# FNet mixing with a squared-ReLU feed-forward: E's coefficients by way of DRAM, weights rounded in two operations

## The chip, the cores and the metric

One Trainium2 chip, one of its cores. The metric is the device time of one execution in microseconds (us); the profile adds one execution taken by the hardware profiler, whose times are those of the tables below. The engines are TensorE (PE for its products, PEld for its weight loads), VectorE (DVE), ScalarE (ACT), GpSimd (POOL) and SyncE (SP), which here only issues transfers.

## The reference

x has 8 sequences of 3008 rows and 256 columns, in float32; w_in is 256 x 2048 and w_out 2048 x 256. Both weights come as float64 arrays, since a float32 array is multiplied by a float64 scalar.

```python
X = np.fft.fft(x, axis=1)
X = np.fft.fft(X, axis=2)
h = X.real.reshape(8 * 3008, 256) @ w_in
g = np.maximum(h, 0.0) ** 2
out = g @ w_out
```

## The kernel before

**The transform.** The real part of the two-dimensional transform is written with symmetries. For each sequence the rows of x are folded and multiplied by cosine and sine tables along the sequence; the results are P (tile Pt) and Q (tile Qt), 128 partitions by 1505 frequencies, where the partitions are half of the 256 columns. The transform along the columns is not carried out on them: it is folded into the weights instead. w_in is multiplied once by the column tables cosd and sind, which gives G1 and G2, 128 x 2048 each, and the first product of the feed-forward is then G1 with P plus or minus G2 with Q: the sum serves a frequency k, the difference its mirror.

**E.** One column of x, the middle one (number 128), does not fit into the 128 partitions. Its transform along the sequence is a single row of 1505 numbers for each sequence, called E (in DRAM as e_dram, spread over all partitions in the tile ew). For each of the 2048 hidden units it needs one coefficient, which is the last partition (127) of G2: row 127 there is w_in summed with alternating signs. The tile gE, 128 x 16, holds these coefficients with the hidden unit on the partition, so that DVE can add E times its coefficient to hP (`front`, L1019, and `front_half`/`split_half`, L1001). To bring row 127 of G2 onto the partitions, `ends_of` (L352) multiplies 128 x 128 pieces of G2 with the last column of the identity, and `keep_ends` (L359) halves the result on DVE into gE (L360). A product in float32 is two instructions for each of two halves of the hidden units: 4 for each of 8 weight groups j, 32 in all.

**Halving and doubling.** gE holds half of each coefficient, and E twice its value. For the first sequence `f_e` (L562) copies the column with a sign of 1 or -1 into `lone`; for the other seven, whose columns are loaded element by element into the tile xe (`load_columns`, L456), POOL doubles xe (L475).

**Rounding the weights.** The weights arrive as float64, as pairs of 32-bit words, and are turned into float32 by `convert` (L289): DVE takes the sign (`begin`, L299), ACT scales the high word (L306) and rounds the low word in two steps (L307 adds 2^23 so that the fraction is rounded away, L308 takes 2^23 off again), DVE shifts the high word (`halves`, L314), and POOL adds the two (`product`, L323). It runs 8 times for w_in, 8 times for w_out and twice more at the end, when two groups of w_out are read anew. The tokens TS, PW, H and PR in the order below are these four parts.

**Steps.** A step is one block of 252 (or 246) frequencies with one group j of 256 hidden units; there are 8 sequences x 6 blocks x 8 groups = 384 steps. A step takes 8 instructions for hP and hQ (L1015), DVE's sum with E and the sum and difference with hQ into g (L1019, L1023, L1024; for the first steps L1001 to L1004), ACT's relu and square (L1028, L1031) and POOL's sums for a fast product with w_out (L1043 to L1060). Two steps later PE multiplies with w_out and with sums of its parts, wsum (`run`, L1080), into six banks F0 to F2 and S0 to S2. After the 8 groups of a block `gather` (L1122) forms the block's output c from the banks: `early` copies a part of F to SBUF on ACT; `upper`, `lower`, `joins` and `last_joins` are sums on DVE, placed between the steps; `back` is a copy on ACT. In the last block (`final`) one sum is formed on POOL instead, and the last two groups are multiplied plainly in `finish` (L1181), which adds them to c (L1191).

**Order.** No scheduler moves anything: each engine runs its instructions in the order in which the program writes them. The first 10 steps, the building of G1, G2 and gE, the rounding of the weights and the sums of w_out are interleaved by a list of tokens written by hand, ORDER (L1423). In it pgC3 and pgD3 are the products for group 3 of G1 and G2, GC3 and GD3 ACT's copies (`keep_win`, L348), fe3 and gE3 the two parts of the coefficients, f3a and f3b the two halves of step 3's first product, d3a and d3b what DVE does with them (L1001, L1003, L1004), rl and sq relu and square, bk the plain product with w_out of the first 8 steps, lc four loads of xe, sc and su the sums of w_out, restP and restQ the rest of P and Q. SP issues its transfers in the same order, among them the raw weights: when the rounding of one (H) has freed its buffer, `load_more` issues the next. A wait on SP holds all that stands behind it. hP and hQ share two banks of PSUM, so that a step's products wait for DVE to have read an earlier one.

A stretch of ORDER that matters for the steps 1, 2 and 6:

```python
'... pgC2 GD1 TSw0 rl0 fe1 f1b H3 PWw0 f1a gE1 PR3 '
'd1b pgD2 GC2 d1a GD2 keep f2b TS4 rl1 pgD3 Hw0 fe2 GD3 pgC3 sq0 gE2 PRw0 d2b ...'
'gE5 PRw3 pgD6 d5b sq3 f5a GC6 H7 lc bk3 GD6 rl4 TSw4 PR7 PWw4 d5a pgD7 restP rl5 fe6 Hw4 f6b GD7 sq4 f6a '
'gE6 PRw4 d6b sq5 sc0a fe7 pgC7 gE7 TSw5 bk4 TSw6 PWw5 restQ GC7 d6a spl lc ...'
```

Of the kernel before, what the change touches and what calls it, by code (L numbers as in the profile page):

```python
# [15 lines left out]
P = 128  # L16
# [68 lines left out]
def kernel(  # L85
# [119 lines left out]
    gE = const.tile([P, NFC], F32, name="gE")  # L205

# [39 lines left out]
    ramp = const.tile([P, 2], F32, name="ramp")  # L246
    nc.vector.memset(ramp[:, 0:1], 2.0 ** 23)
    nc.vector.memset(ramp[:, 1:2], -2.0 ** 23)
# [40 lines left out]
    def convert(raw, dst, k):  # L289
# [12 lines left out]
        def powers():  # L302
            if high is None:
                return
            m = st["m"] = scratch()
            act(high.bitcast(F32), high.bitcast(F32), AF.Copy, scale=2.0 ** -112)  # L306
            act(m, low, AF.Relu, bias=ramp[:, 0:1], scale=2.0 ** -29)  # L307
            act(m.bitcast(U32), m, AF.Relu, bias=ramp[:, 1:2], scale=1.0)  # L308
# [39 lines left out]
    def keep_win(j, side, pg):  # L348
        to, v = (G1, G2)[side].rearrange("p (h j f) -> j p h f", h=2, j=NJ)[j], pg.rearrange("p (h f) -> p h f", h=2)
        nc.scalar.copy(to, v)  # L350

    def ends_of(j):  # L352
        ps = psd.tile([P, CH], F32, name="pe", tag="d")
        for h in range(2):
            fc = j + NJ * h
            nc.tensor.matmul(ps[:, h:h + 1], G2[:, fc * P:(fc + 1) * P], last, start=True, stop=True)
        return ps

    def keep_ends(j, ps):  # L359
        nc.vector.tensor_scalar_mul(gE[:, j::NJ], ps[:, 0:2], 0.5)  # L360
# [99 lines left out]
    def fold_columns():  # L460
# [12 lines left out]
        def begin():  # L473
            assert not COLUMNS
            gt(out=xe, in0=xe, in1=xe, op=ADD)  # L475
# [56 lines left out]
    def fold(t):  # L532
# [28 lines left out]
        def f_e():  # L561
            nc.scalar.mul(lone[r, 2 * t:2 * t + 2, P - 1:], w[r, :, H:H + 1], -1.0 if TILES[t][0] else 1.0)  # L562
# [552 lines left out]
    def gather_plain(n):  # L1115

        c = new_c(n)
        for h, nm in enumerate(("mA", "mB")):
            nc.scalar.copy(c[:, 2 * n * h:2 * n * (h + 1)], acc[nm][:, 0:2 * n])
        return c  # L1120

    def gather(n, final):  # L1122
# [10 lines left out]
        def early():  # L1133
            nc.scalar.copy(cf[:, 1:3], F1[:, 0:2])
            nc.scalar.copy(cf[:, 0], F2[:, 0])

        def upper():
            tt(out=o[:, 3], in0=F0[:, 0], in1=cf[:, 2], op=SUB)
            tt(out=o[:, 4:6], in0=F0[:, 1:3], in1=wide(cf[:, 2:3]), op=ADD)
            tt(out=o[:, 1], in0=F1[:, 2], in1=cf[:, 1], op=ADD)  # L1140
            tt(out=o[:, 2], in0=F1[:, 0], in1=cf[:, 0], op=SUB)
            tt(out=o[:, 0], in0=F2[:, 1], in1=cf[:, 0], op=ADD)

        def lower():
# [5 lines left out]
            if final:  # L1150
                gt(out=cs[:, 0], in0=vt[:, 0], in1=vt[:, 1], op=SUB)
                gt(out=o[:, 4], in0=o[:, 4], in1=cs[:, 0], op=ADD)
# [526 lines left out]
```

## Time and profile before

| | |
|---|---|
| median of 3 runs | 1870.71 us (1870.31 to 1871.78) |
| the profiled execution | 1872.4 us |
| its span, first to last instruction | 1870.6 us |
| granted TensorE clock | 0.998 |
| PE busy | 1856.8 us, 99% |
| DVE busy | 1472.0 us, 79% |
| POOL busy | 1463.9 us, 78% |
| ACT busy | 1086.8 us, 58% |
| products of `ends_of` (L356) | 32, from 33.6 to 78.0 us |
| DVE's copies of gE (L360) | 8, 161 ns (median) |
| ACT's second rounding step (L308) | 18, 722 ns each |
| transfers on SP's queue | 151166 packets, 66.79 MB |

A row of a timeline or a group names engine, line of the program, operation, and the tiles written and read; in square brackets stands the idle time of the engine just before and what ended it. The rows of busy time by stretch name the stretch in us from the start of the span, its length, the busy time and number of instructions of PE, PEld, DVE, ACT and POOL, the granted clock, the mean busy share of the DMA engines and the GB/s that they moved. An engine's busy time counts overlapping instructions once. A transfer's line on SP is its issue; the transfer itself goes on after it.

### The profile page before, as it was taken

To read this page: it belongs to the slowest core of one execution; us is meant where nothing else is said; L and a number is where in the kernel's file an instruction comes from. 1 tells how busy PE (TensorE), PEld (TensorE's weight loads), DVE (VectorE), ACT (ScalarE), POOL (GpSimd) and SP (SyncE) were. 2 spreads that over 40 slices of the span, in tenths; PEclk is the share of its full clock that TensorE was granted. 3 is DMA by queue.
4 is the path that set the end of the run, shared out by engine and by line. 5 is a ranking of instruction groups with operands and counts; after the bars stand their busy time and mean duration, and the time that the engine had idled before them with its cause. 6 is when DMAs were issued, how large, how long until landed. Compare 5 with 4: busy or idle time off the path is not lost.

```text
span 1870.6 us, 34033 instructions
## 1 busy us (share of the span) xinstructions
PE 1856.8 (99%) x11384; PEld 1752.6 (94%) x11384; DVE 1472.0 (79%) x3488; ACT 1086.8 (58%) x1609; POOL 1463.9 (78%) x2140
## 2 busy tenths in 40 slices
PE   9999999999999999999999999999999999999998
PEld 7689999999999999999999999999999999999997
DVE  7788877887788877878787787788877887767666
ACT  5876645666465655566556564566645666444454
POOL 3479878878787887888878887788877878788885
PEclk9999999999999999999999999999999999999999
DMA  7432001100011111111011110111001100000010
GB/s 198 119 55 46 15 21 46 51 23 21 21 51 40 29 23 32 32 46 31 16 32 46 37 26 15 43 48 34 15 20 43 37 15 20 18 20 15 20 43 23
DMA packets 151886, 69.51 MB, mean 37 GB/s; under 512 B 131207, under 2 KB 142945, under 8 KB 151712
## 3 DMA queue, kind: packets, MB, share of 16 engines
q1 hardware_dynamic: 151166, 66.79, 14.4%
q8 instruction: 91, 1.49, 0.3%
q14 instruction: 83, 0.68, 0.1%
q0 software_dynamic: 416, 0.43, 0.1%
q10 hardware_dynamic: 130, 0.12, 0.0%
HBM read 42.59 MB, written 24.69 MB: 36 GB/s over the span
## 4 chain that ended last, share of the span: by engine, by line
PE 95%; DVE 3%; DMA 1%; ACT 1%; issue 0%; POOL 0%; DVEq 0%; POOLq 0%; ACTq 0%
PE F L1080 33%; PE S L1080 23%; PE hP L1015 17%; PE hQ L1015 17%; PE pd L745 2%; PE pd L868 1%; PE pd L842 1%; PE pg L345 1%; DVE wsum L390 0%; DMA cosT<-in_cos_s_dram 0%; PE fin L1188 0%; DVE he L1019 0%; PE mA L1109 0%; PE mB L1109 0%; DVE he L1001 0%
## 5 line engine op out<-in xcount | busy, mean ns | idle before, releaser
L1028 ACT ACTIVATE g<-g 128x1008 f32<-128x1008 f32 (+1 forms) x384 | 399.4, 1040 | 301.7 <-DVE g L1024 280.2
L1019 DVE SCALAR_TENSOR_TENSOR he<-ew,gE,hP 128x252 f32<-128x252 f32 (+1 forms) x748 | 321.4, 471 | 286.5 <-PE hP L1015 286.5
L1031 ACT ACTIVATE g<-g 128x1008 f32<-128x1008 f32 (+1 forms) x384 | 399.4, 1040 | 12.0
L1015 PE MATMUL hP<-Pt,G 128*128 128x252 f32 (+1 forms) x1496 | 379.0, 376 | 3.4 <-DVE w L670 1.4
L1015 PE MATMUL hQ<-Qt,G 128*128 128x252 f32 (+3 forms) x1496 | 379.1, 376 | 0.3 <-DVE g L1024 0.3
L1080 PE MATMUL F<-s,wsum 128*128 128x168 f32 (+1 forms) x1496 | 335.3, 306 | 0.0
L1015 PEld LDWEIGHTS hQ<-Qt,G 128*128 128x128 f32 (+1 forms) x1496 | 281.8, 190 | 37.7 <-issue 2.6
L1080 PE MATMUL F<-g,wout 128*128 128x168 f32 (+1 forms) x1496 | 304.0, 305 | 0.0
L1053 POOL TENSOR_TENSOR s<-g 128x168 f32<-128x168 f32 (+1 forms) x187 | 101.2, 541 | 256.2 <-ACT g L1031 122.4
L1015 PEld LDWEIGHTS hP<-Pt,G 128*128 128x128 f32 x1496 | 265.9, 190 | 22.6 <-DVE fs L606 1.6
L1023 DVE TENSOR_TENSOR g<-he,hQ 128x504 f32<-128x504 f32 (+1 forms) x374 | 253.0, 676 | 41.2 <-DVE he L1019 2.9
L1080 PE MATMUL S<-s,wout 128*128 128x168 f32 (+1 forms) x1496 | 280.6, 306 | 0.1
L1080 PE MATMUL S<-s,wsum 128*128 128x168 f32 (+1 forms) x1496 | 273.7, 306 | 0.4 <-DVE c L1165 0.4
L1080 PE MATMUL F<-g,wsum 128*128 128x168 f32 (+1 forms) x1496 | 273.5, 305 | 0.0
L1024 DVE TENSOR_TENSOR g<-he,hQ 128x504 f32<-128x504 f32 (+1 forms) x374 | 250.7, 670 | 0.0
L1080 PEld LDWEIGHTS S<-s,wsum 128*128 128x128 f32 x1496 | 239.1, 190 | 9.0 <-issue 0.9
L1080 PEld LDWEIGHTS F<-s,wsum 128*128 128x128 f32 x1496 | 247.5, 190 | 0.0
L1080 PEld LDWEIGHTS F<-g,wsum 128*128 128x128 f32 x1496 | 239.3, 190 | 8.1
L1080 PEld LDWEIGHTS F<-g,wout 128*128 128x128 f32 x1496 | 239.3, 190 | 0.0
L1080 PEld LDWEIGHTS S<-s,wout 128*128 128x128 f32 x1496 | 231.0, 190 | 1.0 <-POOL s L1060 0.6
L1059 POOL TENSOR_TENSOR s<-s 128x336 f32<-128x336 f32 (+1 forms) x187 | 168.0, 898 | 14.7
L1056 POOL TENSOR_TENSOR s<-s 128x336 f32<-128x336 f32 (+1 forms) x187 | 168.0, 898 | 14.7
(232 smaller groups left out, 2520.2 us busy)
## 6 DMA issues: line engine op xcount, KB each, us to landing
out_dram<-os SPq DMA_DIRECT2D x376, 56.0 KB
xt<-in_x_dram SPq DMA_DIRECT2D x39, 384.0 KB
xt<-in_x_dram SPq DMA_DIRECT2D x63, 128.0 KB
raw<-in_moe_w_out_dram SPq DMA_DIRECT2D x20, 256.0 KB
ew<-e_dram SPq DMA_DIRECT2D x39, 126.0 KB
out_dram<-os SPq DMA_DIRECT2D x288, 7.0 KB
raw<-in_moe_w_in_dram SPq DMA_DIRECT2D x16, 256.0 KB
xt<-in_x_dram SPq DMA_DIRECT2D x2, 512.0 KB
```

Of the source, the lines that this page charges most:

```text
L345: nc.tensor.matmul(pg, tab[:, i], win[j][:, i], start=i == 0, stop=i == 1)
L745: nc.tensor.matmul(ps[0:w.shape[-1]], w, part_of(cosT if lone_e else tab, t)[0:rows, kp, PLACE[t]:PLACE[t] + NC[kp][c]], start=t == ts[0] ...
L1015: nc.tensor.matmul(to[:, h, 0:n], w[:, fs], v[:, ks], start=h == 0, stop=True, skip_group_check=True)
L1019: nc.vector.scalar_tensor_tensor(out=t[:, h, 0:n], in0=window[b, k0][:, 0:n], scalar=gE[:, fc:fc + 1], in1=hP[:, h, 0:n], op0=ALU.mult, op ...
L1023: tt(out=g[:, :, 0:n], in0=t[:, :, 0:n], in1=hQ[:, :, 0:n], op=ALU.add)
L1024: tt(out=g[:, :, n:2 * n][:, :, ::-1], in0=t[:, :, 0:n], in1=hQ[:, :, 0:n], op=ALU.subtract)
L1028: act(g[:, :, 0:2 * n], g[:, :, 0:2 * n], AF.Relu)
L1031: act(g[:, :, 0:2 * n], g[:, :, 0:2 * n], AF.Square)
L1053: gt(out=s[:, 11], in0=b2[:, 0], in1=b1[:, 0], op=SUB)
L1056: gt(out=s[:, 4:6], in0=s[:, 4:6], in1=s[:, 10:11].to_broadcast([P, 2, tb]), op=SUB)
L1059: gt(out=s[:, 6:9:2], in0=s[:, 2:4], in1=s[:, 6:8], op=ADD)
L1080: nc.tensor.matmul(acc[nm][:, slot, 0:tb], w, v, start=q == 0 and nm not in begun, stop=q == end - 1, skip_group_check=True)
```

## The change

Row 127 of G2 no longer goes through TensorE. After ACT's copy of a group of G2, SP writes the group's 256 coefficients from that partition to a small array in DRAM, g_dram, and then reads them back with the hidden unit on the partition, straight into gE (`take_ends`). `ends_of` and `keep_ends` go. In ORDER the read stands right behind the copy: "GD1 gE1".

gE is no longer halved, so E is: `f_e` copies with 0.5 or -0.5, and POOL's doubling of xe goes.

The rounding takes two operations of ACT: L307 writes the rounded low word as an integer at once, without taking 2^23 off. The sum with the high word is then one binary exponent too high, so the weights are twice as large. w_in's factor of two is taken out in the copies of G1 and G2, w_out's where the block's output is gathered: ACT's copies there are scaled by 0.5, and DVE's sums with a bank of PSUM become SCALAR_TENSOR_TENSOR, which halves one operand and adds. The last block takes the same way through `gather` as the others.

```diff
@@ -203,6 +203,7 @@
     G1 = const.tile([P, F], F32, name="G1")
     G2 = const.tile([P, F], F32, name="G2")
     gE = const.tile([P, NFC], F32, name="gE")
+    g_dram = dp.tile([NJ, 2 * P], F32, name="g_dram")
 
     def load_table(tab, src, tiles, queue=nc.sync):
@@ -243,9 +244,9 @@
     for c in range(2):
         nc.vector.tensor_scalar(out=sind[:, c, P - 1:], in0=evens, scalar1=2.0, scalar2=-1.0,
                                 op0=ALU.mult, op1=ALU.add)
-    ramp = const.tile([P, 2], F32, name="ramp")
-    nc.vector.memset(ramp[:, 0:1], 2.0 ** 23)
-    nc.vector.memset(ramp[:, 1:2], -2.0 ** 23)
+    ramp = const.tile([P, 1], F32, name="ramp")
+    nc.vector.memset(ramp, 2.0 ** 23)
+    FACTOR = 2.0 if moe_w_in.dtype != F32 else 1.0
 
 
     def awake(n):
@@ -304,8 +305,7 @@
                 return
             m = st["m"] = scratch()
             act(high.bitcast(F32), high.bitcast(F32), AF.Copy, scale=2.0 ** -112)
-            act(m, low, AF.Relu, bias=ramp[:, 0:1], scale=2.0 ** -29)
-            act(m.bitcast(U32), m, AF.Relu, bias=ramp[:, 1:2], scale=1.0)
+            act(m.bitcast(U32), low, AF.Relu, bias=ramp, scale=2.0 ** -29)
 
         def halves():
             if high is None:
@@ -347,17 +347,13 @@
 
     def keep_win(j, side, pg):
         to, v = (G1, G2)[side].rearrange("p (h j f) -> j p h f", h=2, j=NJ)[j], pg.rearrange("p (h f) -> p h f", h=2)
-        nc.scalar.copy(to, v)
-
-    def ends_of(j):
-        ps = psd.tile([P, CH], F32, name="pe", tag="d")
-        for h in range(2):
-            fc = j + NJ * h
-            nc.tensor.matmul(ps[:, h:h + 1], G2[:, fc * P:(fc + 1) * P], last, start=True, stop=True)
-        return ps
-
-    def keep_ends(j, ps):
-        nc.vector.tensor_scalar_mul(gE[:, j::NJ], ps[:, 0:2], 0.5)
+        nc.scalar.mul(to, v, 1.0 / FACTOR)
+        if side:
+            nc.sync.dma_start(out=g_dram[j:j + 1].rearrange("o (h f) -> o h f", h=2),
+                              in_=G2[P - 1:P].rearrange("o (h j f) -> j o h f", h=2, j=NJ)[j])
+
+    def take_ends(j):
+        nc.sync.dma_start(out=gE[:, j::NJ], in_=g_dram[j].rearrange("(h f) -> f h", h=2))
 
     def weights(D, row):
 
@@ -472,7 +468,6 @@
 
         def begin():
             assert not COLUMNS
-            gt(out=xe, in0=xe, in1=xe, op=ADD)
             s = hp.tile([P, 2, NL, NE], F32, name="es", tag="es", bufs=1)
             gt(out=s, in0=xe[:, 0::2], in1=xe[:, 1::2], op=ADD)
             for kp in range(2):
@@ -559,7 +554,7 @@
                 tt(out=w[r, kp, part], in0=v[r, 0, part], in1=v[r, 1, part], op=SUB if kp else ADD)
 
         def f_e():
-            nc.scalar.mul(lone[r, 2 * t:2 * t + 2, P - 1:], w[r, :, H:H + 1], -1.0 if TILES[t][0] else 1.0)
+            nc.scalar.mul(lone[r, 2 * t:2 * t + 2, P - 1:], w[r, :, H:H + 1], -0.5 if TILES[t][0] else 0.5)
 
         return [f_s, f_d, f_sc, f_dc, lambda: (f_w(PART[0]), f_e()), lambda: f_w(PART[1])]
 
@@ -1116,10 +1111,13 @@
 
         c = new_c(n)
         for h, nm in enumerate(("mA", "mB")):
-            nc.scalar.copy(c[:, 2 * n * h:2 * n * (h + 1)], acc[nm][:, 0:2 * n])
+            nc.scalar.mul(c[:, 2 * n * h:2 * n * (h + 1)], acc[nm][:, 0:2 * n], 1.0 / FACTOR)
         return c
 
-    def gather(n, final):
+    def scaled(out, in0, in1, op=ADD):
+        mix(out=out, in0=in0, scalar=1.0 / FACTOR, in1=in1, op0=ALU.mult, op1=op)
+
+    def gather(n):
 
         tb = 2 * n // 3
         c = new_c(n)
@@ -1131,15 +1129,15 @@
         wide = lambda v: v.to_broadcast([P, 2, tb])
 
         def early():
-            nc.scalar.copy(cf[:, 1:3], F1[:, 0:2])
-            nc.scalar.copy(cf[:, 0], F2[:, 0])
+            nc.scalar.mul(cf[:, 1:3], F1[:, 0:2], 1.0 / FACTOR)
+            nc.scalar.mul(cf[:, 0], F2[:, 0], 1.0 / FACTOR)
 
         def upper():
-            tt(out=o[:, 3], in0=F0[:, 0], in1=cf[:, 2], op=SUB)
-            tt(out=o[:, 4:6], in0=F0[:, 1:3], in1=wide(cf[:, 2:3]), op=ADD)
-            tt(out=o[:, 1], in0=F1[:, 2], in1=cf[:, 1], op=ADD)
-            tt(out=o[:, 2], in0=F1[:, 0], in1=cf[:, 0], op=SUB)
-            tt(out=o[:, 0], in0=F2[:, 1], in1=cf[:, 0], op=ADD)
+            scaled(out=o[:, 3], in0=F0[:, 0], in1=cf[:, 2], op=SUB)
+            scaled(out=o[:, 4:6], in0=F0[:, 1:3], in1=wide(cf[:, 2:3]), op=ADD)
+            scaled(out=o[:, 1], in0=F1[:, 2], in1=cf[:, 1], op=ADD)
+            scaled(out=o[:, 2], in0=F1[:, 0], in1=cf[:, 0], op=SUB)
+            scaled(out=o[:, 0], in0=F2[:, 1], in1=cf[:, 0], op=ADD)
 
         def lower():
 
@@ -1147,9 +1145,6 @@
             nc.scalar.copy(cs, S0[:, 0:2])
             tt(out=vt[:, 0:2], in0=S1[:, 0:2], in1=cs, op=ADD)
             tt(out=vt[:, 2:4], in0=S2[:, 0:2], in1=vt[:, 0:2], op=ADD)
-            if final:
-                gt(out=cs[:, 0], in0=vt[:, 0], in1=vt[:, 1], op=SUB)
-                gt(out=o[:, 4], in0=o[:, 4], in1=cs[:, 0], op=ADD)
             tt(out=S1[:, 2], in0=S1[:, 2], in1=vt[:, 3], op=ADD)
             tt(out=S0[:, 0:2], in0=vt[:, 3:1:-1], in1=S0[:, 0:2], op=SUB)
             tt(out=vt[:, 4], in0=vt[:, 2], in1=S1[:, 2], op=SUB)
@@ -1158,16 +1153,14 @@
             nc.scalar.copy(S1[:, 1], vt[:, 1])
 
         def joins():
-            tt(out=o[:, 3::-2], in0=o[:, 3::-2], in1=S0[:, 0:2], op=ADD)
+            scaled(out=o[:, 3::-2], in0=S0[:, 0:2], in1=o[:, 3::-2])
             tt(out=S0[:, 2], in0=S0[:, 2], in1=vt[:, 4], op=ADD)
-            if not final:
-                tt(out=S1[:, 1], in0=vt[:, 0], in1=S1[:, 1], op=SUB)
-            tt(out=o[:, 2::3], in0=o[:, 2::3], in1=wide(S0[:, 2:3]), op=ADD)
+            tt(out=S1[:, 1], in0=vt[:, 0], in1=S1[:, 1], op=SUB)
+            scaled(out=o[:, 2::3], in0=wide(S0[:, 2:3]), in1=o[:, 2::3])
 
         def last_joins():
-            tt(out=o[:, 0], in0=o[:, 0], in1=S1[:, 2], op=ADD)
-            if not final:
-                tt(out=o[:, 4], in0=o[:, 4], in1=S1[:, 1], op=ADD)
+            scaled(out=o[:, 0], in0=S1[:, 2], in1=o[:, 0])
+            scaled(out=o[:, 4], in0=S1[:, 1], in1=o[:, 4])
 
         return c, (early, upper, lower, back, joins, last_joins)
 
@@ -1188,7 +1181,7 @@
                     nc.tensor.matmul(ps[:, 0:2 * n], wout[:, j, h, a], g[:, a, 0:2 * n], start=j < NJ - 1 and a == 0,
                                      stop=j == NJ - 1 and a == 1)
             for at in (slice(0, 2 * n),) if h == 0 else (slice(n, 2 * n), slice(0, n)):
-                tt(out=v[:, h, at], in0=ps[:, at], in1=v[:, h, at], op=ADD)
+                scaled(out=v[:, h, at], in0=ps[:, at], in1=v[:, h, at])
         spans = {s: span(b, k0, n, s) for s in (1, 0)}
         po = {s: psd.tile([P, 2, H, 2], F32, name="po", tag="d") for s in (1, 0)}
         for h in range(2):
@@ -1330,6 +1323,7 @@
     awake(5)
     for a in range(2):
         keep_win(0, a, dft_win(0, a))
+    take_ends(0)
     folds_of("P3")
     products_of("P2 P3")
     p_part("copy")
@@ -1349,7 +1343,6 @@
     p_part("keep")
     q_part("copy")
     products_of("Q5")
-    ends = ends_of(0)
     second = round_win(1, raw["in", 1])
     second[0]()
     second[1]()
@@ -1363,7 +1356,6 @@
     for nm in ("join_4", "join_2"):
         groups[1, 1, nm]()
     q_part("lo")
-    keep_ends(0, ends)
     BLOCKS = [(k0, min(CK, NKT + 1 - k0)) for k0 in range(0, NKT, CK)]
     assert all(n % 3 == 0 for _, n in BLOCKS)
     steps = [(b, k0, n, j) for b in range(B) for k0, n in BLOCKS for j in range(NJ)]
@@ -1421,12 +1413,12 @@
 
     ROUNDED = ['3', 'w0', '4', 'w1', '5', 'w2', '6', 'w3', '7', 'w4', 'w5', 'w6', 'w7']
     ORDER = (
-        'sp TS2 f0a et TS3 PW2 pgD1 d0a pgC1 H2 f0b GC1 PW3 PR2 d0b pgC2 GD1 TSw0 rl0 fe1 f1b H3 PWw0 f1a gE1 PR3 '
-        'd1b pgD2 GC2 d1a GD2 keep f2b TS4 rl1 pgD3 Hw0 fe2 GD3 pgC3 sq0 gE2 PRw0 d2b f2a GC3 PW4 fe3 d2a f3b sq1 '
-        'bk0 TSw1 H4 PWw1 PR4 TS5 Hw1 pgD4 f3a GD4 gE3 PW5 PRw1 d3b pgC4 d3a fe4 rl2 bk1 GC4 TSw2 H5 PWw2 PR5 gE4 '
-        'pgD5 TS6 Hw2 f4b GD5 sq2 f4a d4b PRw2 PW6 fe5 pgC5 d4a bk2 GC5 TSw3 H6 PWw3 PR6 TS7 rl3 pgC6 Hw3 PW7 f5b '
-        'gE5 PRw3 pgD6 d5b sq3 f5a GC6 H7 lc bk3 GD6 rl4 TSw4 PR7 PWw4 d5a pgD7 restP rl5 fe6 Hw4 f6b GD7 sq4 f6a '
-        'gE6 PRw4 d6b sq5 sc0a fe7 pgC7 gE7 TSw5 bk4 TSw6 PWw5 restQ GC7 d6a spl lc PWw6 Hw5 su0a f7b PRw5 f7a sc1a TSw7 '
+        'sp TS2 f0a et TS3 PW2 pgD1 d0a pgC1 H2 f0b GC1 PW3 PR2 d0b pgC2 GD1 gE1 TSw0 rl0 f1b H3 PWw0 f1a PR3 '
+        'd1b pgD2 GC2 d1a GD2 gE2 keep f2b TS4 rl1 pgD3 Hw0 GD3 gE3 pgC3 sq0 PRw0 d2b f2a GC3 PW4 d2a f3b sq1 '
+        'bk0 TSw1 H4 PWw1 PR4 TS5 Hw1 pgD4 f3a GD4 gE4 PW5 PRw1 d3b pgC4 d3a rl2 bk1 GC4 TSw2 H5 PWw2 PR5 '
+        'pgD5 TS6 Hw2 f4b GD5 gE5 sq2 f4a d4b PRw2 PW6 pgC5 d4a bk2 GC5 TSw3 H6 PWw3 PR6 TS7 rl3 pgC6 Hw3 PW7 f5b '
+        'PRw3 pgD6 d5b sq3 f5a GC6 H7 lc bk3 GD6 gE6 rl4 TSw4 PR7 PWw4 d5a pgD7 restP rl5 Hw4 f6b GD7 gE7 sq4 f6a '
+        'PRw4 d6b sq5 sc0a pgC7 TSw5 bk4 TSw6 PWw5 restQ GC7 d6a spl lc PWw6 Hw5 su0a f7b PRw5 f7a sc1a TSw7 '
         'bk5 Hw6 PWw7 su1a d7b PRw6 rl6 d7a sq6 f8b Hw7 sc2a f8a rl7 su2a d8b sq7 PRw7 d8a sc3a sc1b bk6 rl8 su3a hi8 su1b '
         'f9a sq8 f9b df d9a cm8 sc2b d9b sc0b rl9 hi9 su2b sq9 bk7 cm9 '
     ).split()
@@ -1501,10 +1493,8 @@
             made[what, nm] = dft_win(int(nm), int(what == "pgD"))
         elif what in ("GC", "GD"):
             keep_win(int(nm), int(what == "GD"), made["pg" + what[1], nm])
-        elif what == "fe":
-            made["fe", nm] = ends_of(int(nm))
         elif what == "gE":
-            keep_ends(int(nm), made["fe", nm])
+            take_ends(int(nm))
         elif what in "fd":
             i, h = int(nm[:-1]), int(nm[-1] == "b")
             if what == "f":
@@ -1588,9 +1578,9 @@
             if not last_half:
                 first_half(q, n_, made["g", at], made["g", at + 1], made["s", group], hook, end)
                 if q == end - 1:
-                    c_, ops = gather(n_, final)
+                    c_, ops = gather(n_)
                     gather_next = ops[0]
-                    pending += [(i + 1, ops[1])] + ([] if final else [(i + 2, ops[3])]) + [(i + 2, ops[4])]
+                    pending += [(i + 1, ops[1]), (i + 2, ops[3]), (i + 2, ops[4])]
                     lower = ops[2]
                     if final:
                         last_c = c_
```

## The prediction

> **What bounds the kernel now.** I read the page first (busy time, the chain of waits), then busy time by stretch, then the timelines of single engines where a stretch is full. From the page, parts 1 and 4:
>
> ```profile
> PE 1856.8 (99%) x11384; PEld 1752.6 (94%) x11384; DVE 1472.0 (79%) x3488; ACT 1086.8 (58%) x1609; POOL 1463.9 (78%) x2140
> PE 95%; DVE 3%; DMA 1%; ACT 1%; issue 0%; POOL 0%; DVEq 0%; POOLq 0%; ACTq 0%
> ```
>
> TensorE is the chain nearly throughout. By stretch (length; then busy time of PE, PEld, DVE, ACT and POOL):
>
> ```profile
> 34.00:62.00 28.00, 27.13 (x116) 19.87 (x117) 19.44 (x50) 22.70 (x39) 10.44 (x8) 1.00 0.33 100
> 62.00:80.00 18.00, 17.86 (x72) 12.36 (x71) 13.07 (x32) 17.14 (x27) 5.64 (x5) 1.00 0.43 112
> 80.00:111.00 31.00, 29.41 (x119) 20.04 (x117) 30.11 (x76) 23.12 (x43) 19.67 (x23) 1.00 0.36 52
> 300.00:1800.00 1500.00, 1500.00 (x9369) 1439.80 (x9368) 1181.72 (x2778) 860.28 (x1236) 1207.87 (x1765) 1.00 0.12 30
> ```
>
> The change lives in the first three rows. From 34 to 80 PE is full and DVE has room; from 80 to 111 DVE is full (30.11 of 31.00), so what makes DVE late near 78 us stays lost, up to the point (111.6) from which PE alone runs to the end. From 300 to 1800 PE has no gap.
>
> **32 products removed (fe).** They are 8 stretches of 4; one of them:
>
> ```profile
> 62.40 0.59 PE L988 MATMUL ph<-Qt,G 127*128 127x252 f32 x2
> 62.83 0.50 PE L356 MATMUL pe<-ident,G 128*128 128x1 f32 x4
> 63.19 1.11 PE L345 MATMUL pg<-win,cosd 128*128 128x256 f32 x4
> ```
>
> 63.19 - 62.83 is 0.36 us of PE's queue, and the product behind it takes 1.11 where its like takes 1.03: 0.44 each, 3.5 us in all, lying at 33.6, 41.9, 47.0, 49.2, 56.4, 62.8, 75.6 and 77.7 us. DVE loses 8 L360 (0.1 each in its queue).
>
> **One of three rounding operations removed.** 18 of L308:
>
> ```profile
> L308 ACT ACTIVATE m<-m,ramp 128x512 uint32<-128x512 f32 x18 | 13.0, 722 | 0.6
> ```
>
> 13.0 us of ACT, 0.65 to 0.8 each in its queue (66.55 to 67.18; 65.75 to 66.55 for the step before it). ACT is nearly full only from 62 to 80 (17.14 of 18.00), and there PE waits once for it (0.16 at 71.1). So it is worth about 0.2 us of PE, and it pulls G's second copy of step 1 forward.
>
> **The round trip added.** Each of 8 coefficients now takes a write (SP, 2 x 512 B from one partition) that waits for ACT's copy of G2, and a read (SP, 256 elements of 4 B) that waits for the write: 16 DMAs on SP's queue, and DVE's L1001 waits for the read. For the write, SP's two lines at 101 us, the second of which waits for the first:
>
> ```profile
> 101.50 0.25 SPq L979 DMA_DIRECT2D e_dram<-Qt  x1
> 102.83 0.35 SPq L964 DMA_DIRECT2D ew<-e_dram  x1
> ```
>
> So 1.33 us for 2.9 KB from one partition. The read is bounded by xe's loads of 224 such elements: the trace's semaphore events have them landing 1.7 us after issue when alone and 2.9 behind a 126 KB load. I take 1.75, nearest to the lone ones, and 3.1 us for a free trip. The Trainium skill (DMA: Bandwidth & Descriptors, "Anatomy of one DMA", told of the other path) puts a fixed cost of about 2.0 us on each DMA; by it a trip would be 4.0 and everything below 0.9 later, but the write's row says 1.33.
>
> Step by step against L1001's times now. **Step 0**: written at about 19, behind loads that land until 28; SP stands until then, so load 3 goes at 29 in place of 25.74. It is used at 36.2, others later: hidden. **Step 1**: G2's copy is at 41.46 now; without one L308 and the first 0.36 it ends at 40.75, the trip at 43.9. L1001 was at 43.47, and PE, 0.8 ahead, waits about 1.3 for a bank of PSUM. **Step 2**: copy done at 44.75, its write behind weight load 5 (42.7 to 46.1 by then), read at 48.0 against 47.74; PE waits 0.3. PE has by then given back all it gained (-0.8 -0.4 -0.4 +1.6), and gains again: -0.3 at 57, -0.75 at 64, -1.4 at f6b, -1.8 at 78. **Steps 3, 4, 5, 7**: trips end at about 53, 59.7, 65.7 and 83 against needs at 53.5, 61.5, 68.7 and over 86: on time, step 3 barely. The weight loads moved behind them start up to 2 us later and are used 6 us or more after that.
>
> **Step 6** is the one that costs. In the order by hand the write stands behind `lc`, four loads of x's column, which stand behind the last weight load:
>
> ```profile
> 71.36 0.81 SPq L285 DMA_DIRECT2D raw<-in_moe_w_out_dram  x2
> 72.27 4.35 SPq L456 DMA_DIRECT2D xe<-in_x_dram  x4
> ```
>
> SP is held to 76.62, and the queue's transfers are not done even then (last two columns: DMA share, GB/s):
>
> ```profile
> 77.00:78.00 1.00, 1.00 (x9) 0.90 (x7) 0.89 (x3) 1.00 (x3) 0.00 (x0) 1.00 0.35 10
> 79.00:80.00 1.00, 1.00 (x4) 0.51 (x4) 1.00 (x4) 1.00 (x2) 0.00 (x0) 1.00 0.08 16
> ```
>
> The four land until 79.5. So the write ends between 76.65 + 1.31 = 78.0 (it overtakes) and 79.6 (it queues), the read 1.75 later, 79.7 to 81.4. The Trainium skill (same page, "Why a DMA increments its semaphore by 16 and not by 1") says that a transfer uses the largest number up to 16 that divides its slowest dimensions, on the lowest-numbered engines, each in ring order: five for 95 rows, two for the write, so the same ones. The loads' six semaphore events (five engines and one jump) agree; by this rule alone it is the late end. All of it starts 0.75 earlier than now, since load and `lc` wait for DVE's L314 after d5b, which PE brings forward by that: 79.0 to 80.7, and I take 80.0. Where DVE stands now:
>
> ```profile
> 76.11 0.16 DVE L360 TENSOR_SCALAR gE<-pe 128x2 f32<-128x2 f32 x1 [2.06 <-PE pe L356]
> 77.08 0.48 DVE L1001 SCALAR_TENSOR_TENSOR he<-ew,gE,ph 128x252 f32<-128x252 f32 x1 [0.80 <-PE ph L988]
> ```
>
> L1001 slips from 77.08 to 80.0, +2.9. Queued behind it on DVE are two L299 (ACT's rounding of w5 and w6 waits for them), Qt's two L786 (POOL's write of e_dram waits), d6a, and the sums of wout; PE waits for PSUM from f7b on. Of the 0.9 that DVE idles from 80 to 111 some 0.4 absorbs, and L360 at 78.27 is gone (0.1): **+2.4** at 111.6. Without the stall DVE would have started 1.4 early: that gain is gone too.
>
> **The gathering.** In 47 blocks 9 TENSOR_TENSOR become SCALAR_TENSOR_TENSOR with a constant, and `early` scales. No row has that operation in fp32 with a constant. L314 (constant, integers) takes 0.68 for 512 where L606, a plain sum, takes 0.68: +0.01. L1019 (a scalar per partition) takes 0.471 for 252 where L1003 takes 0.417: +0.054. I take 0.01, by the constant. What it must stay under: PE's next S group reuses the bank that L1165 reads.
>
> ```profile
> 1015.97 0.50 DVE L1165 TENSOR_TENSOR c<-c,S 128x336 f32<-128x336 f32 x1
> 1016.95 0.45 PE L1080 MATMUL S<-s,wsum 128*128 128x168 f32 x2
> ```
>
> 0.48 from end to start, of which 0.14 is hand-over (seen where PE waits for it, at 1838.45): 0.34 of cover in 38 blocks, 0.23 in others. Seven operations lie ahead of that end: 0.07 is covered; 0.38 is not, and would cost 0.04 x 38 + 0.15 x 8 = 2.7 us. At 1830 to 1838.45 DVE is the chain: +0.07. ACT's scaled copies: +0.02 by L562's scale (0.21) against a copy (0.19); cf is ready 2 us early, G's copies lie in ACT's room.
>
> **The end.** The last block loses two POOL operations and gains two DVE (0.24 each) and an ACT copy (0.30). They hide here:
>
> ```profile
> 1863.85 0.73 DVE L1191 TENSOR_TENSOR c<-fin,c 128x246 f32<-128x246 f32 x2 [2.57 <-PE fin L1188]
> ```
>
> DVE is idle 2.57 us there; without that they would cost 0.7. On the path is the first L1191 with its constant: +0.01 to 0.05. POOL's doubled xe (0.56 at 148.7) goes, off the path.
>
> **The sum.** +2.4 (step 6) + 0.07 + 0.05 = +2.5 us. The profiled execution took 1872.4 (span 1870.6, 1.8 around it): 1874.9. That is 1.7 above the median of the runs shown; against the median, 1870.71 + 2.5 = **1873.2**. A measurement of this kernel can tell about 0.2% (3.7 us) from no change, so this is no change, on the slow side.
>
> **Rivals.** (A) *TensorE's products count*: coefficient 6 is there by 75.7, DVE enters its full stretch 1.4 early and all of it is kept: -1.4 - 0.1 = -1.5, 1869.2. For it: PE gains 3.5 us in the queue that is the chain. Against it: SP reaches the write only at 75.9, and a trip takes 3.1. It decides if `lc` is much shorter when it starts earlier. (B) *The gathering stalls PE*: a constant costs what L1019's scalar costs, L1165 ends past its cover in every block: +2.5 + 2.7 = 1875.9. For it: L1019 is the only fp32 row of the kind; against it: its scalar lies in memory. It decides from 0.05 per operation. (C) *The trips are longer*, the slow side: the write queues to 79.6 and the read takes the 2.9 of the loaded row, so L1001 of step 6 stands at 81.8 and not 80.0, and steps 3 and 4, with 0.5 and 1.8 to spare, come late behind weight loads too, which takes PE's gain (0.75 at most) and delays `lc` with it: 1873.2 + 1.8 + 0.75 = 1875.8. It decides from a trip of some 4 us; for it speaks that all of it shares one queue with loads of 256 KB.
>
> **How the numbers follow.** Forecast 0.50 (its own range 1871.6 to 1874.9, by the two ends of step 6 and 0.3 for the rest), A 0.16, B 0.12, C 0.19, else 0.03. The range runs from below A to past B and C, with B and C together at the top: 1868.6 to 1878.3. Faster by over 0.2% (under 1867.0) is beyond A: 0.04. Slower (over 1874.4) takes a fifth of the forecast and most of B and C: 0.10 + 0.11 + 0.15 = 0.36. The rest, 0.60, is within 0.2%.
>
> **What would show it.** Step 6: L1001 near 80 with an idle time of some 4 us ended by a DMA of gE; SP's write of g_dram behind four L456 at about 76; DVE's last full stretch ending near 114. Step 1: a wait for gE of about 1.3 at 43 to 44. TensorE: no L356, the stretch 34 to 75 shorter by 1.4. Rounding: 18 fewer ACTIVATE, and no longer two rows. Gathering: L1138 to L1170's successors within 0.02 of now, and PE full from 300 to 1800; a gap before every S group means B. I am wrong if L1001 of step 6 starts before 77, if another step's wait is longer than step 6's, or if PE shows gaps in the steady part.

## The result, and the profile after

The changed kernel takes 1874.48 us (median of 11 runs, 1874.06 to 1876.46) against 1870.66 us for the kernel before (11 runs, 1869.82 to 1871.78). That is 3.8 us more between the medians. The ratio over all the runs is 1.0023, its 95% interval 1.0015 to 1.0031: a slowdown clear of zero, which lies just on the 0.2% that the prediction took as the limit of "no change". The profiled execution of the changed kernel took 1874.34 us, with a span of 1872.2.

The page of the changed kernel, busy time and the chain of waits by engine:

```profile
PE 1855.4 (99%) x11352; PEld 1751.2 (94%) x11352; DVE 1471.8 (79%) x3481; ACT 1074.7 (57%) x1592; POOL 1460.3 (78%) x2137
PE 94%; DVE 1%; DMA 1%; ACT 1%; POOL 0%; SPq 0%; issue 0%; DVEq 0%; POOLq 0%; ACTq 0%
```

TensorE has 32 products fewer and 1.4 us less to do, ScalarE 12.1 us less, and the time is longer all the same: what an engine has to do says little here, what it waits for says all. Busy time by stretch, in the same four stretches as in the prediction:

```profile
34.00:62.00 28.00, 24.77 (x98) 17.97 (x97) 19.96 (x46) 18.80 (x34) 9.62 (x7) 1.00 0.43 130
62.00:80.00 18.00, 17.98 (x60) 10.83 (x58) 9.26 (x20) 12.29 (x20) 5.60 (x4) 1.00 0.41 99
80.00:111.00 31.00, 27.53 (x99) 18.89 (x99) 29.83 (x77) 20.33 (x31) 17.34 (x20) 0.89 0.35 49
300.00:1800.00 1500.00, 1500.00 (x9365) 1440.15 (x9364) 1181.58 (x2781) 862.10 (x1236) 1206.75 (x1767) 1.00 0.12 30
```

From 34 to 62 TensorE now has 3.2 us of gaps where it had 0.9; from 62 to 80 DVE does 9.3 us of work in place of 13.1, since it stands still for 7 us; from 300 to 1800 TensorE is full, as before. Where DVE stood still, on its timeline (first operations of steps 1, 5 and 6):

```profile
43.38 0.48 DVE L996 SCALAR_TENSOR_TENSOR he<-ew,gE,ph 128x252 f32<-128x252 f32 x1 [2.71 <-DMA gE<-g_dram]
...
68.14 0.48 DVE L996 SCALAR_TENSOR_TENSOR he<-ew,gE,ph 128x252 f32<-128x252 f32 x1 [1.52 <-PE ph L983]
...
79.76 0.47 DVE L996 SCALAR_TENSOR_TENSOR he<-ew,gE,ph 128x252 f32<-128x252 f32 x1 [7.01 <-DMA gE<-g_dram]
```

and SP's timeline from 66 us on, in the same execution:

```profile
66.71 4.16 SPq L286 DMA_DIRECT2D raw<-in_moe_w_out_dram  x4
70.91 4.41 SPq L452 DMA_DIRECT2D xe<-in_x_dram  x4
75.41 1.06 SPq L352 DMA_DIRECT2D g_dram<-G  x1
77.59 0.40 SPq L356 DMA_DIRECT2D gE<-g_dram  x1
```

Step 6's group of G2 had been copied by ScalarE at 69.38. Its write goes at 75.41, directly behind the four loads of xe; the read goes at 77.59 and DVE starts at 79.76. So the coefficient is ready on chip 10 us before DVE gets it, and 6 of these are spent behind other transfers on one queue.

Nothing of the kind is seen in the gathering. A sum with S in the new form, in the changed kernel:

```profile
L1118 DVE SCALAR_TENSOR_TENSOR c<-S,c 128x336 f32<-128x336 f32 x78 | 39.1, 501 | 0.0
```

501 ns, where the plain sums of that shape in the kernel before (L1161, L1165) took 497 on average.

**The first profile of the kernel before was a late one.** The kernel before was profiled once more (1871.0 us, span 1869.2). 

> The kernel before, unchanged, for a second profiled execution. The first one was 1.5 us above the median of its runs and shows a granted clock of 0.74 from 12 to 18 us. Theory: the sums were made against an execution that was late by itself, and in this one DVE's last full stretch ends (TensorE's hP behind L606) some 0.5 to 1.5 us before 111.62, which is the part of the 3.6 us that the first pair of profiles does not show. Rival: it ends at 111.62 within 0.2, and the rest lies behind it.

Measured: the first execution was 1.31 us behind from before 41 us on (its product of G at L345 began at 40.89, in the second at 39.58) and kept this to the end (1.33 at the join, which is the end of DVE's last full stretch, where TensorE's hP stops waiting for DVE: 111.62 against 110.29; 1.39 at the end). It came from a lost clock. TensorE had stood idle for 1.57 us up to 13.23, and from 14.93 to 18.34 its granted clock was one half: its products of G at L345, which take 1.13 and 1.03 us in the second execution, took 1.91 and 1.51, and what began 0.10 behind the second execution at 15.66 was 1.33 behind at 18.72. The stretch in the first execution, and in the second (granted clock third from the right):

```profile
12.00:18.00 6.00, 4.77 (x24) 4.35 (x25) 5.79 (x14) 1.99 (x5) 2.65 (x3) 0.74 1.06 307
12.00:18.00 6.00, 4.68 (x30) 4.31 (x31) 5.79 (x14) 2.56 (x7) 2.35 (x3) 1.00 1.06 299
```

The same steps as above, on DVE's timeline of this second execution:

```profile
42.16 0.48 DVE L1001 SCALAR_TENSOR_TENSOR he<-ew,gE,ph 128x252 f32<-128x252 f32 x1 [0.80 <-PE ph L988]
...
68.12 0.48 DVE L1001 SCALAR_TENSOR_TENSOR he<-ew,gE,ph 128x252 f32<-128x252 f32 x1 [1.62 <-PE ph L988]
...
75.76 0.48 DVE L1001 SCALAR_TENSOR_TENSOR he<-ew,gE,ph 128x252 f32<-128x252 f32 x1 [0.80 <-PE ph L988]
```

So the change moved step 1 by 1.2 us, step 5 by nothing and step 6 by 4.0, and the join by 4.02 (110.29 to 114.31). This is the pair to compare; the first pair shows only 2.7 at the join, because a late execution before stands beside a usual one after.

### The profile page after: what moved, and what is told of

Same layout as the page of the kernel before. It is cut to its first block, busy times and chain, and to the rows that moved or that the text cites. A ratio compares the mean times of both kernels' runs of the same rounds, so it can differ in the third digit from the quotient of the medians.

```text
span 1872.2 us, 33957 instructions
## 1 busy us (share of the span) xinstructions
PE 1855.4 (99%) x11352; PEld 1751.2 (94%) x11352; DVE 1471.8 (79%) x3481; ACT 1074.7 (57%) x1592; POOL 1460.3 (78%) x2137
## 4 chain that ended last, share of the span: by engine, by line
PE 94%; DVE 1%; DMA 1%; ACT 1%; POOL 0%; SPq 0%; issue 0%; DVEq 0%; POOLq 0%; ACTq 0%
PE F L1075 33%; PE S L1075 22%; PE hP L1010 17%; PE hQ L1010 16%; PE pd L863 1%; PE pd L837 1%; PE mA L1104 1%; PE pd L740 1%; PE mB L1104 1%; PE pg L345 0%; PE ph L981 0%; PE ph L983 0%; PE fin L1181 0%; DMA g_dram<-G 0%; DVE he L1014 0%
```

## The experiments

The theory to be tested: the loss is step 6's write standing behind `lc` on SP's queue. The rivals: the gathering or the rounding costs it; the trips cost it at every step.

**One part alone.** products_kept has the rounding, the halved copies and the scaled gathering of the changed kernel, and the coefficients by TensorE's products as before (`ends_of`, `keep_ends`, the old ORDER and E doubled again). trip_only is the opposite: the kernel before, with E halved in place of gE and with the trip (lines cut):

```diff
+            nc.sync.dma_start(out=g_dram[j:j + 1]..., in_=G2[P - 1:P]...)
-    def ends_of(j):
-    def keep_ends(j, ps):
+    def take_ends(j):
-            gt(out=xe, in0=xe, in1=xe, op=ADD)
```

and the changed ORDER. 

> The changed kernel with the coefficients by TensorE's 32 products again, as before; the rounding in two operations, the scaled copies of G and the scaled gathering stay. Theory: step 6 stands as before, the rounding gives TensorE 0.2 us and the gathering takes 0.1: 1870.2 to 1871.0, no difference from before. Rival 1 (gathering or rounding costs it): 1873 to 1874.5. Another outcome, that ACT's room pulls DVE's full stretch forward by more than 0.5 us, would give 1869 to 1870.

> The kernel before with the trip through DRAM alone, in the changed order; rounding in three operations, plain copies and plain gathering as before. Theory: the loss is that of the changed kernel, L1001 of step 6 near 80, 1873.8 to 1875.0 (ACT has less room, so up to 0.5 more). Rival 1 (gathering or rounding costs it): 1870 to 1871.

Measured: products_kept 1870.26 us (ratio 0.9996, interval 0.9987 to 1.0004; kernel before 1870.92), join at 109.81. trip_only 1877.34 us (1.0035, 1.0023 to 1.0048), join at 116.36, with this on DVE's timeline:

```profile
81.55 0.48 DVE L997 SCALAR_TENSOR_TENSOR he<-ew,gE,ph 128x252 f32<-128x252 f32 x1 [6.80 <-DMA gE<-g_dram]
```

All of the loss is in the trip; gathering and rounding cost nothing. But trip_only came out 2.9 us above the changed kernel, where at most 0.5 more was expected. In the profiled executions that is 2.05 at the join and 1.2 between there and the end of the span (0.67 of it from the last store on, see below), less 0.3 outside the span. ScalarE's copies of G stand behind its roundings: with the third operation back, step 1's write goes at 40.27 in place of 39.51, and step 6 starts 1.8 us later. About half of this 1.8 goes with a lost clock (below): in trip_only_kept_busy, which keeps its clock there, step 6 starts at 80.60, 0.8 us behind the changed kernel. So the rounding in two operations is worth 0.5 us at the join when TensorE makes the coefficients, and some 0.8 us at step 6 when a trip hangs on the copy.

**The place in the queue.** In lc_behind one token of ORDER moves, in write6_before_loads one pair:

```diff
 lc_behind
-f5a GC6 H7 lc bk3 GD6 gE6 rl4 ... GD7 gE7 sq4
+f5a GC6 H7 bk3 GD6 gE6 rl4 ... GD7 gE7 lc sq4
 write6_before_loads
-f5a GC6 H7 lc bk3 GD6 gE6 rl4
+f5a GC6 GD6 gE6 H7 lc bk3 rl4
```

> The changed kernel with one token of the order by hand moved: lc, the four loads of x's column, stands behind gE7 (step 7's coefficients) in place of before bk3 and gE6. Theory (the loss comes from step 6's write standing behind lc on SP): the write goes at about 71 us in place of 75.41, L996 of step 6 starts when its products are there, at about 75 in place of 79.76, PE's gap of 3.02 us at 83 goes, the join of DVE and PE after the full stretch is near 110.3 in place of 114.31, and the time is 1869.3 to 1870.5. Rival 1 (the gathering and the rounding cost it, step 6's wait is covered elsewhere): 1874 to 1874.5, the join earlier but no shorter time. Rival 2 (the trips as such, steps 1 and 2 as much as 6): step 6's wait shrinks but the time stays at 1872 to 1873.

> The changed kernel with GD6 and gE6 moved ahead of H7, so that step 6's write and read stand ahead of the weights' load and of lc; lc itself stays where it is, ahead of step 7's trip. Theory (the place on SP's queue, not lc's load on the DMA engines, made step 6 late): L996 of step 6 at 75 or earlier in place of 79.76, 1870.3 to 1871.0 as lc_behind, and step 7's trip, now the one behind lc, lands at about 80, still ahead of its need at 83 to 84. Rival (step 7's takes the place of step 6's): step 7's L996 waits for its transfer, and 1872 to 1873.5.

Measured: lc_behind 1870.75 us (1.0000, 0.9991 to 1.0008), step 6 at 75.58, join at 109.98. write6_before_loads 1869.75 us (0.9996, 0.9988 to 1.0005; kernel before 1870.7), join at 109.50. SP's timeline of write6_before_loads, and below it DVE's:

```profile
69.55 0.64 SPq L352 DMA_DIRECT2D g_dram<-G  x1
71.23 0.38 SPq L356 DMA_DIRECT2D gE<-g_dram  x1
71.66 0.93 SPq L286 DMA_DIRECT2D raw<-in_moe_w_out_dram  x2
72.70 4.30 SPq L452 DMA_DIRECT2D xe<-in_x_dram  x4
77.04 1.04 SPq L352 DMA_DIRECT2D g_dram<-G  x1
```

```profile
75.09 0.48 DVE L996 SCALAR_TENSOR_TENSOR he<-ew,gE,ph 128x252 f32<-128x252 f32 x1 [2.19 <-PE ph L983]
```

The write goes 6 us earlier, DVE waits for TensorE's products and not for a transfer, and 4.7 us are back, a little more than expected. `lc` is as long as before (4.30), and the trip that now stands behind it, step 7's, is needed at 83.74 and on time. So it is the order on the queue, not the load on the DMA engines. The rival that every trip costs alike falls here too: steps 1 and 2 wait in both runs as in the changed kernel (2.72 and 0.53 us of DVE in lc_behind), and yet the time is that of the kernel before. In lc_behind the write still stood behind the weights' loads until 71.23, and step 6 waited 2.49 us for it; with the write ahead of those too, that wait went.

**The other trips.** lc_and_early_GD1 adds an earlier copy for step 1, trips_early also one for step 2, and step 6's write ahead of the loads:

```diff
 lc_and_early_GD1, on top of lc_behind
-pgC1 H2 f0b GC1 PW3 PR2 d0b pgC2 GD1 gE1 TSw0
+pgC1 H2 GD1 gE1 f0b GC1 PW3 PR2 d0b pgC2 TSw0
 trips_early, on top of that
-d0b pgC2 TSw0 rl0 f1b H3 ... d1b pgD2 GC2 d1a GD2 gE2 keep
+d0b pgC2 pgD2 TSw0 rl0 GD2 gE2 f1b H3 ... d1b GC2 d1a keep
-GC6 H7 bk3 GD6 gE6 rl4
+GC6 GD6 gE6 H7 bk3 rl4
```

> lc behind gE7 as in the run lc_behind, and ACT's copy of step 1's G2 with its trip (GD1 gE1) moved ahead of GC1 and PW3, to directly behind H2. Theory: the write goes at about 37.2 in place of 39.5, the coefficients land at 41.0 in place of 43.4, TensorE's gap of 1.78 us at 43 to 44.8 shrinks to 0.3 or less. If TensorE keeps this through 62 to 80 and DVE's full stretch starts earlier by it, 1.0 to 1.5 less than lc_behind: 1868 to 1869.3. Rival: the weights' loads or ACT hold the stretch from 62 to 80, and it is the same as lc_behind within 0.3.

> lc_and_early_GD1 with two more moves in the order by hand: step 2's pgD2, GD2 and gE2 directly behind pgC2 and rl0, and step 6's GD6 and gE6 ahead of H7, so that its write does not stand behind the weights' loads. Theory: the trips of steps 1, 2 and 6 are all back before their products, TensorE has no gap from 40 to 98 but the one at 39.9, and DVE's full stretch starts 2 to 2.6 us earlier than with the 32 products: join at 107.3 to 108 in place of 109.81, time 1867.8 to 1868.8, better than both kernels. Rival: the weights' loads, ACT or POOL hold the stretch from 48 to 75, and it is 1869.5 to 1870.3, no better than products_kept.

Measured: lc_and_early_GD1 1870.31 us (0.9996, 0.9987 to 1.0005), and not the 1868 to 1869.3 expected: step 1 no longer waits for its coefficient, but step 2 then does (2.46 us of DVE), and TensorE's gap of 1.78 at 43 is one of 1.98 at 47.3. The wait moved one step on. With step 2's trip early too, trips_early takes 1868.12 us (1867.76 to 1869.11; 0.9988, 0.9979 to 0.9997; kernel before 1870.3). On DVE's timeline:

```profile
42.86 0.48 DVE L996 SCALAR_TENSOR_TENSOR he<-ew,gE,ph 128x252 f32<-128x252 f32 x1 [1.52 <-PE ph L983]
46.76 0.48 DVE L996 SCALAR_TENSOR_TENSOR he<-ew,gE,ph 128x252 f32<-128x252 f32 x1 [0.34 <-DMA gE<-g_dram]
...
74.25 0.48 DVE L996 SCALAR_TENSOR_TENSOR he<-ew,gE,ph 128x252 f32<-128x252 f32 x1 [2.19 <-PE ph L983]
```

Step 6 starts at 74.25, the join is at 108.67, 1.6 ahead of the kernel before. It beats both kernels by 2.2 and 6.4 us, with the same arithmetic as the changed one. It is less than a join of 107.3 to 108 would have been: small waits at 44 and 48 us (0.59 and 0.22 of TensorE) are left, and step 3 waits 0.72 us for its transfer.

**The lost clock.** The changed kernel's runs form three groups, at 1874.1 to 1874.5, 1875.3 to 1875.5 and 1876.3 to 1876.5. In the profiled execution of lc_and_early_GD1 (1871.47, one of its slowest; the others go down to 1869.27) TensorE stood idle from 47.3 to 49.3, and then (granted clock third from the right):

```profile
50.00:52.00 2.00, 2.00 (x5) 1.05 (x4) 2.00 (x6) 1.12 (x2) 0.38 (x1) 0.63 0.10 9
52.00:54.00 2.00, 2.00 (x3) 0.68 (x2) 1.97 (x3) 0.22 (x1) 1.30 (x2) 0.52 0.44 127
```

Four pairs of the plain products with w_out, which begin 0.85 us apart otherwise, took from 50.23 to 55.31: 5.1 us in place of 3.4, at a place where TensorE is the bound. Three runs put products on the identity, whose results nothing uses, into such gaps, so that TensorE does not stand idle:

```diff
+        elif what == "idle":
+            filled = psd.tile([P, CH], F32, name="filled", tag="d")
+            for _ in range(int(nm)):
+                nc.tensor.matmul(filled[:, 0:P], ident, ident, start=True, stop=True)
 after_kept_busy:        keep idle7 f2b, su0a idle12 f7b
 trip_only_kept_busy:    keep idle10 f2b
 early_GD1_kept_busy:    d2a idle7 f3b
```

> The changed kernel with plain products on the identity (128x128, results unused) where TensorE stands idle: 7 before step 2's second half (gap of 1.78 us at 43) and 12 before step 7's (3.02 at 80). They change no wait. Theory (a gap of 2 to 3 us costs TensorE its clock in some executions, and the drop costs up to 2 us where TensorE is the bound): no granted clock under 1 from 44 to 92, the runs at 1875.3 and 1876.4 go, all within 1874.1 plus or minus 0.4. Rival (the spread has another cause, such as the transfers): the same three groups from 1874.1 to 1876.4.

> trip_only with 10 such products before step 2's second half, where its TensorE stood idle for 2.71 us and then ran at half clock from 46 to 50. Theory: clock 1.00 there, 1.5 to 1.8 us less than trip_only's 1877.3: 1875.5 to 1875.9. Rival (the lost clock is hidden behind DVE's wait at step 6): 1877.3.

> lc_and_early_GD1 with 7 products on the identity (0.24 us each, results unused) in TensorE's gap of 1.98 us at 47.3, before step 3's second half. In the profiled execution of lc_and_early_GD1 the granted clock was 0.63 and 0.52 from 50 to 54 behind that gap, where TensorE is the bound, and four products of mA and mB took 1.7 us more. Theory (the lost clock makes the spread of 1869.3 to 1872.0): all runs at 1869.3 to 1869.9, median 0.4 to 0.8 under lc_and_early_GD1's 1870.31, the clock 1.00 from 44 to 62. Rival (the spread comes from the start, before 38 us, as in the first profile of the kernel before): the same spread, no lower median.

Measured: after_kept_busy 1873.86 us (1.0018, 1.0009 to 1.0027), ten runs from 1873.08 to 1874.25 and one at 1875.68. Four of them lie below the 1874.1 plus or minus 0.4 expected, and the one above it; 0.3 of the 0.6 between the medians of the changed kernel and this one lies outside the span (2.1 us around it there, 1.8 here). The one above was the profiled execution: its clock is 1.00 from 44 to 92, and it was already 1.55 us behind the changed kernel's execution at 40.86, before any of the gaps. A load of x had come late, at full clock. DVE began the operation that waits for it 1.54 us later than in the changed kernel's execution (21.08):

```profile
22.62 0.69 DVE L536 TENSOR_TENSOR fs<-xt 120x512 f32<-120x512 f32 x1 [1.40 <-DMA xt<-in_x_dram]
```

The other two runs: early_GD1_kept_busy 1869.99 us (0.9997, 0.9988 to 1.0006), from 1869.31 to 1870.54: the lowest is that of lc_and_early_GD1, the highest 1.45 lower, the median only 0.3. trip_only_kept_busy 1877.47 us (1.0037, 1.0025 to 1.0050): nothing gained in the median. The clock is 1.00 from 44 to 62 and step 6 stands at 80.60 in place of 81.55, but then the clock was lost behind another gap, of 3.24 us at 81.4, and of the 0.95 us only 0.43 are left at the join (115.93).

With the products in the gaps the late runs become fewer: 1 of 11 in place of 5 in the changed kernel, and none over 1870.6 in place of 4 in lc_and_early_GD1. That makes a lost clock a likely cause of them, and not more. The loss of clock that the changed kernel's profile shows, behind the gap of 3.02, is not what makes its slower groups, since this execution (1874.34) is one of the lowest group. And there is a second cause, the late load of x. The medians move by 0.3 to 0.6 us, inside the intervals, and the changed kernel without any loss of clock from 44 to 92 is still slower than the kernel before (1.0009 to 1.0027): the lost clock is no cause of the 3.8 us. What it costs in trip_only stays open: step 6 came 0.95 us earlier without it, and the median did not fall.

## Why the prediction was right or wrong

**The mechanism was right.** Slower by little, by step 6, through SP's queue: undoing that one place alone (write6_before_loads) takes back the whole loss.

Two of the positions agree by luck. L1001 of step 6 was foreseen near 80 and the end of DVE's full stretch near 114, and they came at 79.76 and 114.31. But both were counted on the first, late execution; counted on a usual one, 1.31 earlier, they would stand at 78.7 and 112.7, and the changed kernel is 1.1 and 1.6 behind that. The idle time ahead of step 6 was put at some 4 us and is 7.01: the 2.06 and 0.80 us for which DVE stood there in the kernel before come on top of the slip.

**Its size was short: 1873.2 forecast, 1874.5 measured, +2.5 against +3.8.** The measured time lies as far below rival C's 1875.8 as above the forecast. It lies in the forecast's own range, 1871.6 to 1874.9; the ends that the prediction gives for it (step 6 at 79.0 or 80.7, and 0.3 for the rest) come to 1871.9 to 1874.2, and outside of that. (B and C together are 1878.5 by their terms, not 1878.3.) "No change" was close: 1874.4 was its upper end. Two terms were mis-sized, a third had the wrong sign, and a fourth was left out.

- *The free trip, put at 3.1 us.* Step 1's write was issued at 39.51, its read at 41.22, and DVE started at 43.38: 3.87 us. The write alone is 1.7 (1.33 was taken from the write of 2.9 KB), the read 2.2 (1.75 was taken from xe's lone loads). The Trainium skill's fixed cost (DMA: Bandwidth & Descriptors, "Anatomy of one DMA"), told of the other path, gave an estimate of 4.0 for the two transfers, and the trace, with 3.87, sides with it. Step 1 is late by that, and the lead of 0.75 us that TensorE was to have by step 5 is gone: its gap at step 1 is 1.78 in place of 1.3, that at step 2 0.40 in place of 0.3, and 0.17 more passes before its product at 66.11. Step 5 stands at 68.14 against 68.12, and `lc` begins at 70.91 against 70.95 in the second profile of the kernel before. The forecast had step 6's write 0.75 earlier than that. With it, L1001 of step 6 slips by 4.0 us and not by 2.9. From write to DVE, 4.1 us behind `lc` were foreseen and 4.35 measured.
- *What DVE would absorb, put at 0.5.* It absorbed nothing: from step 6's first operation to the join it takes 34.55 us in the changed kernel (79.76 to 114.31) and 34.53 in the kernel before (75.76 to 110.29). Over all the runs this stretch takes from 34.40 to 35.50. The idle time in that stretch stands behind TensorE and ScalarE, which slip with it.
- *The end, put at +0.01 to +0.05.* From the first product of `fin` to the end the changed kernel takes 12.98 us, the kernel before 13.64: 0.66 less.
- *The time outside the span, taken as 1.8 us as in the kernel before.* It is 2.1 in every run of the changed kernel: 0.34 more, of which the traces show no cause.

By these, 4.0 at the join, 0.4 given back between there and the first product of `fin` (its cause is open), and 0.66 at the end leave 3.0 between the spans of the usual executions (1869.2 to 1872.2). The medians stand 0.8 further apart: 0.34 by the time outside the span, and 0.48 because the kernel before was profiled 0.34 above its median and the changed kernel 0.14 below.

**The sum was anchored rightly.** The lateness of the first profile was left in the trace on both sides, and the sum was put on the median; so its 1.31 us did not get into the forecast, though it hid as much of the loss in the first pair of profiles.

**Step 1 and step 2** waited, as told, 2.71 and 0.52 us of DVE. **Steps 3, 4, 5 and 7** were on time, **step 0** hidden. **The rounding** was put at 0.2 us of TensorE: by products_kept 0.48 at the join and unresolved in the time. Its larger worth beside a trip (some 0.8 us at step 6, from trip_only_kept_busy) was not foreseen. **The gathering** was put at 0.01 us for an operation: 0.004 measured.

**Not foreseen: the stall passes through ScalarE to TensorE.** The prediction had ACT's rounding wait for DVE, and TensorE for a bank of PSUM from step 7 on. TensorE waited for a copy of G; PE's and ACT's timelines of the changed kernel:

```profile
83.03 1.21 PE L981 MATMUL ph<-Pt,G 128*128 128x252 f32 x2 [3.02 <-ACT G L350]
84.03 1.05 PE L983 MATMUL ph<-Qt,G 127*128 127x252 f32 x2
```

```profile
81.39 0.67 ACT L307 ACTIVATE raw<-raw 128x512 f32<-128x512 f32 x1 [4.36 <-DVE fd L300]
81.95 0.75 ACT L308 ACTIVATE m<-raw,ramp 128x512 uint32<-128x512 uint32 x1
82.60 0.37 ACT L350 ACTIVATE G<-pg 128x256 f32<-128x256 f32 x1
```

The copy stands behind a rounding, the rounding waits for L300 on DVE, and L300 stands behind step 6's sums: one late transfer stops three engines. It costs little more, and so does the half clock behind that gap (products of 0.43 us took 0.84), since DVE is the bound there: from step 6 to the join it takes 34.55 us, where lc_behind, which has neither, takes 34.40.

**The rivals.** A (the products count, 1869.2) is what happens once the trips are out of the way: trips_early takes 1868.1. Its condition, that `lc` be shorter, was not met: 4.41 against 4.35. B (the gathering stalls TensorE) is refuted by products_kept and by 1500.00 of 1500.00. C (longer trips, 1875.8) was right in its condition, a trip of some 4 us, and wrong in its place: step 6 did not come later by a slower trip behind `lc`, and steps 3 and 4 were not late. Its second part, that TensorE's gain goes and `lc` begins no earlier, came true, but by step 1: there the length told.

## What to carry to other kernels

What TensorE makes in 0.44 us is replaced by a trip through DRAM of 3.9 us with nothing else between its write and its read on the queue. So in this kernel it pays only where the trip starts 4 us ahead of its need; what decides is not the bytes but what stands ahead of the write on its queue. When a transfer is added to a hand-written order, move its issue up to its producer and ahead of every load that waits for something, and then look again at the next step, for the wait moves on. Take a second profile of the kernel before when the first lies above its median: a lateness of 1.3 us in one trace hid a third of the difference.

## What the runs showed of the hardware

**The clock.** In five of the profiled executions TensorE's granted clock fell to one half between their start and their end, each time for 3.41 us or for twice that. The gap is TensorE's idle time ahead of the fall or around it; the last column is what TensorE worked in the 3.41 us before the fall.

| | half clock, us | gap, us | busy before, us |
|---|---|---|---|
| kernel before, first profile | 14.93 to 18.34 | 1.57 | 1.84 |
| lc_and_early_GD1 | 50.52 to 53.93 | 1.98 | 1.43 |
| trip_only | 46.23 to 49.65 | 2.71 | 0.70 |
| changed kernel | 82.17 to 88.99 | 3.02 | 1.26 |
| trip_only_kept_busy | 83.50 to 90.32 | 3.24 | 1.29 |

It kept the clock behind gaps of 1.78 and 1.79, and once behind 3.02 (trip_only at 85.56), so the length of a gap alone does not decide. Where the gap lies may bear on it: counted in steps of 3.41 us from trip_only's own changes of clock, its gap of 3.02 is split over two steps (80.37 to 83.78 and on to 87.19), in which TensorE worked for 2.17 and 1.63 us. That does not settle it either, for a fall followed 1.84 us of work. The Trainium skill (TensorE: Matmul & The Clock Gate, "What's actually happening") tells of a free-running window of some 3.4 us, and of half the clock after at least one idle window. The half clock and the 3.41 us agree; if an idle window is one without work, the 0.70 to 1.84 us of work before each fall do not.

**The last store.** ScalarE's issue of the last store takes 0.63 us in the changed kernel and 1.56 in the kernel before; ACT's queue in the second profile of the kernel before, and in the changed kernel:

```profile
1865.07 1.56 ACTq L1207 DMA_DIRECT2D out_dram<-os  x1
```

```profile
1868.66 0.63 ACTq L1200 DMA_DIRECT2D out_dram<-os  x1
```

products_kept and trips_early show 0.63 too, both with the new closing of the gathering, and trip_only, with the old, 1.67. From this issue to the end of the span it is 3.57 us in the changed kernel and 4.16 in the kernel before, 0.59 of the 0.66 us of the end. With the new closing ScalarE has one copy more some 7 us before the store and stands idle for 5.4 us ahead of its last copies, where it stood idle for 8.6. Whether that is why was not tried.
